# Layer two's mixing: a third block product computed as seven, with its kept sums made earlier in the kernel

## The chip, the core and the metric

The kernel runs on one core of a Trainium2 chip. The metric is the device time of one execution in microseconds (us); lower is better. The core has five engines with an instruction stream each: TensorE (PE, with weight loads shown as PEld), VectorE (DVE), ScalarE (ACT), GpSimd (POOL) and SyncE (SP), which here only issues DMAs. An engine runs its instructions in the order of the program and waits, where it must, for what another engine or a DMA delivers.

## The reference

Two layers, each a linear-attention block and a gated MLP that mixes over tokens, on x of 2048 tokens by 512:

```
def _A_ref(x, wqkv, wo):                      # 32 heads of 16
    qkv = (x @ wqkv) as (3, heads, tokens, 16)
    pq, pk = phi(q), phi(k)                   # t + 1 or exp(t), + 1e-6
    kv = einsum("bhsd,bhse->bhde", pk, v)
    z = einsum("bhsd->bhd", pk)
    o = einsum(pq, kv) / (einsum(pq, z) + 1e-6)
    return o @ wo

def _B_ref(x, w_in, w_sp, b_sp, w_out):       # F = 1792, Fh = 896
    z = gelu(x @ w_in)
    z1, z2 = z[..., :Fh], layernorm(z[..., Fh:])
    g = einsum("ts,bsf->btf", w_sp, z2) + b_sp[None, :, None]
    return (z1 * g) @ w_out

x = A_x
x = x + _A_ref(layernorm(x), A_wqkv, A_wo)
x = x + _B_ref(layernorm(x), B_w_in, B_w_sp, B_b_sp, B_w_out)
x = x + _A_ref(layernorm(x), A_wqkv, A_wo)
x = x + _B_ref(layernorm(x), B_w_in, B_w_sp, B_b_sp, B_w_out)
```

The costliest part is the mixing, `w_sp` (2048 x 2048) times `z2` (2048 x 896), once in each layer, with the same `w_sp`.

## The kernel before

**Arithmetic.** Each fp32 factor is split into a high part (a copy on ACT, `high`, L105) and a low part (a subtraction on DVE, `low`, L108), and a product is three matmuls: high by high, high by low, low by high (`mm3`, L119 to L121; in the mixing L1389 to L1391, and L1329, L1331 and L1332 in a nested product).

**Storage.** On-chip memory is cut into slots: 22 "pages" of 128 x 512 floats (`pg`), six "quads" four times as large (`qd`), four "bigs" (`bg`), tagged pages `z0` to `z15`, and eight accumulator banks. A slot is taken from a list of free ones and given back; whoever takes it next waits until its last reader is done.

**Order.** The program is scheduled by hand: each engine runs its instructions in the order of the code. Loops are over steps, and each step's code names the side work that it takes along. SP issues most DMAs, in order; the loads of kept sums are issued by POOL (L1193).

**Stages**, for each layer: the attention half (`P1`, steps of one token tile of 128), a transition and first half of the MLP (`P2`), the mixing, then the output loop `o` (16 steps, one token tile each, `z1 * g` times `w_out`), which in layer one also prepares layer two's start (`join`: loads of layer two's wk and wq, and of its first turned tiles, `turn.load`). The output tile is added on DVE and stored at L1515.

**The mixing as seven products.** The 2048 x 2048 by 2048 x 896 product is cut two by two, and instead of eight block products seven are computed, P1 to P7, whose operands are sums of blocks and whose results are added into the output. The list `ORDERS` gives the order for each layer. A plain product takes 8 steps, one for each 128 rows of the contraction: in P4, P1 and P5 (`WITH3`) a step has 24 matmuls, in P6, P7 and P3 it has 18. Each step needs one weight tile (fetched four steps ahead by `fetch`, split two steps ahead in `prepare`, ACT L1244 and DVE L1253) and one z tile (built in `operand`, split three steps ahead; L1257). When a product ends, `evac` adds its banks into the output or moves them (for instance L1443, six additions after P7).

**A nested product** ("N") is one of the block products taken once more as seven. N1 stands for P1 and N2 for P2; such a product has 14 steps with 12 matmuls. Seven sub-products (`NEST`) have two steps each. Those in `OWN` load a raw weight tile of 512 KB by SP and split it like the others; those in `SUM` load a sum of weight tiles that was computed earlier, split into high and low, and stored in device memory: 1 MB each, eight in one nested product. `nested_operand` takes its z side, from sums of z tiles made by `token_sums` (L1274, L1275) and others; the PSUM results are added into the output on DVE at each second step.

**Kept sums.** `Inner` makes these, in 16 units for a nested product. A unit is an addition or subtraction of two pages of raw weight (DVE, L1131 to L1141), then a high and a low part, then two stores of 256 KB each. Raw pages are loaded ahead by `Inner.fetch`. Two of these objects, N1 and N2, are served at named steps of `P2.run` and of the mixing (`MIX_UNITS`). The plain products' weight sums are made by another object on POOL (L1050) in layer one.

**Gates.** When a part of the output is complete it goes on the list `ready`; `gates` then loads a page of z1, and one step later multiplies it in on POOL (L1411). POOL also issues the sum loads, in the order of the code.

In layer one the order is P4, P1, P6, P7, P5, P3, N2; in layer two P4, P6, P7, N1, N2, P5, P3.

Of the kernel before, what the change touches and what calls it, by code (L numbers as in the profile page):

```python
# [29 lines left out]
MIX_UNITS = (11, 15, 18, 20, 25, 31, 36, 40), (7, 9, 11, 13, 15, 17, 19, 21)  # L30
# [3 lines left out]
class Slots:  # L34
# [16 lines left out]
    def put(self, *tiles):  # L51
        for t in tiles:
            n, _ = self.held.pop(id(t))
            self.free_list.append(n)


@with_exitstack
def mixer_kernel(ctx: ExitStack, tc: tile.TileContext, x_in, wqkv, wo_d, win1_d, win2_d, wsp_d, bsp_d, wout_d,
# [242 lines left out]
    class P1:  # L301
# [194 lines left out]
        def run(self):  # L496
            side = deque()
            for w in (self.wo, self.win2):
                side.extend([w] * len(w.pieces))
            self.wv = quads.get([P, 4, 512])  # L500
            ND = NT - DEFER
            for s in range(1, NT + 2):
                self.loadx(s + 3)
                self.turn.load(s + 1)
                turned = 2 <= s < NT and s not in self.turn.by_pe
                if turned:
                    self.T_high(s)
                if s == 1:
                    if not self.kb:
                        self.K(0)  # L510
                    self.K(1)
                elif 2 < s <= NT:
                    self.K(s - 1)
                self.ln_a(s + 2)
                if turned:
                    self.T_low(s)
                if s <= NT:
                    self.K_phi(s - 1)
                if s <= ND:
                    self.Q(s - 1)  # L520
                if s == NT + 1:
                    self.late()
                if s <= NT:
                    self.xsplit(s - 1)
                    self.K_split(s - 1)
                if s + 1 < NT and s + 1 in self.turn.by_pe:
# [8 lines left out]
                if s <= 4:  # L535
                    c = s - 1
                    nc.sync.dma_start(self.wv[:, c, :], wqkv[c * P:(c + 1) * P, 1024:1536])
                else:
                    for _ in range(min(len(side), 1 if s < 6 else 2)):
                        side.popleft().piece()  # L540
                if s >= 4:
                    for w in list(side)[:1 if s < 5 else 2]:
                        w.fetch()
# [72 lines left out]
    class P2:  # L616
# [309 lines left out]
        def run(self, sums):  # L926
            w1 = self.win1
            own = inner["N1" if self.seven else "N2"]
            for s in range(1, NT + 3):
# [28 lines left out]
                else:  # L958
# [19 lines left out]
                    if s <= NT + 1:  # L978
                        if not sooner:
                            self.d_high(s - 2)  # L980
                        if 6 <= s < 13 if self.seven else 14 <= s < 18:
                            own.unit()
                        self.d_low(s - 2)
# [87 lines left out]
    class Inner:  # L1071
# [3 lines left out]
        def __init__(self, base):  # L1075
            self.base = base
            self.d = {m: dram.tile([2, P, 2, 2, 512], F32, name=f"n{base}_{m}") for m in range(1, 5)}
# [4 lines left out]
            self.free = None  # L1082

        def part(self):
            if self.free is None:
                return pages.get(PAGE, F32R)
            i = self.free.popleft()
            self.free.append(i)
            return ztag(i, PAGE, "part", F32R)

        def fetch(self):

            if self.ahead:
                k, u = self.ahead.popleft()
                b = self.base
                at = (((3, b), (3, b + 4)), ((2, b),), (), ((2, b + 4),))[u]
                for name, (n, s) in zip(("21", "22") if u == 0 else ("11",) if u == 1 else ("12",), at):
                    self.raw[name] = load(wsp_d[n, s + k])

        def out(self):  # L1100
            for m, k, n, p in self.parts:
                nc.sync.dma_start(self.d[m][k // 2][:, k % 2, n, :], p.bitcast(F32))
                if id(p) in pages.held:
                    pages.put(p)
            self.parts = []

        def finish(self, late=False):
# [7 lines left out]
            if not keep:  # L1115
                pages.put(t)
            self.parts = [(m, k, n, p) for n, p in enumerate((h, l))]
# [31 lines left out]

        def begin(self, n, ahead=2):  # L1150
# [6 lines left out]
    class P4:  # L1157
# [4 lines left out]
        ORDERS = ("P4", "P1", "P6", "P7", "P5", "P3", "N2"), ("P4", "P6", "P7", "N1", "N2", "P5", "P3")  # L1162
# [4 lines left out]
        OWN = {"P1": (2, 0), "P2": (2, 4), "P4": (3, 4)}  # L1167
        SUM = {"P3": 4, "P5": 1, "P6": 2, "P7": 3}

        def __init__(self, p2, sums):  # L1170
# [11 lines left out]
            self.wout = {}  # L1182
            self.wraw = deque()
            self.wsteps = (48, 50, 51, 53, 55, 56, 57) if self.nest_late else range(60, 67)
            self.wloads = (45, 47, 48, 50, 52, 53, 54) if self.nest_late else range(60, 67)

        def fetch(self, g):
# [8 lines left out]
            if p[0] == "N":  # L1196
                n, s = self.OWN[self.NEST[k // 2]]
                s += 2 * (k % 2) + inner[p].base
# [8 lines left out]
        def operand(self, g):  # L1207
# [6 lines left out]
            if p == "P6":  # L1214
                return a[:, H2], -1.0, None
# [60 lines left out]

        def nested_operand(self, g):
            p, d = self.steps[g]
            name, q, base = self.NEST[d // 2], d % 2, inner[p].base
# [16 lines left out]
        def nested_low(self, g):  # L1296
# [7 lines left out]
            for o in range(2):  # L1304
                a, b = (ztile[inner[self.steps[g][0]].base + 2 * q + o + i] for i in (0, 4))
# [7 lines left out]
        def nested_mm(self, g):  # L1313
# [24 lines left out]
            V = nc.vector  # L1338
            for i in range(2):
# [21 lines left out]
            if name == "P4" and self.nest_late:  # L1361
                self.ready.extend((n, f, False) for n in (2, 3) for f in range(4))
# [56 lines left out]
        def evac(self, p):  # L1419
# [3 lines left out]
            if p in ("P4", "P1", "P5"):  # L1423
                for j in range(2):
                    n = 2 + j if p == "P1" else j
                    held = p == "P5"
# [4 lines left out]
            for j in range(2):  # L1431
                a, b = 2 + j, j
                for f in range(3):
# [8 lines left out]
                    elif p == "P7":  # L1442
                        V.tensor_sub(self.unit(b, 4 + f), bs[b], q)  # L1443
# [9 lines left out]
                    if p in ("P4", "P7", "P3"):  # L1453
                        banks.put(q)
            if self.L == 0:
# [24 lines left out]
        def wpiece(self, f):  # L1480
            r = self.wraw.popleft()
            h, l = (main.tile(PAGE, F32R, tag=f"z{2 * f + i}", bufs=1, name=f"wo{self.L}_{f}_{i}") for i in range(2))
# [5 lines left out]
        def loadx(self, i):  # L1488
            if i < NT:
                self.x[i] = load(xs[2 * self.L + 1, i])  # L1490

        def zsplit(self, i):
            if i >= NT:
                return
            n, k = divmod(i, 4)
# [5 lines left out]
        def o(self, i):  # L1501
# [7 lines left out]
            if self.L == 1 and i == NT - 1:  # L1509
# [11 lines left out]
        def run(self, nxt):  # L1521
# [16 lines left out]
            for m in ("N1", "N2"):  # L1538
                if (m, 0) in self.steps:
                    at = self.steps.index((m, 0))  # L1540
                    for k, g in enumerate(range(at - 3, at + 1) if m == "N1" or self.nest_late
                                          else (self.steps.index(("N1", s)) for s in (5, 6, 8, 9))):
                        sums_at[g] = m, k
            for g in range(n):
# [12 lines left out]
                if g == units[0] - 2:  # L1557
                    own.begin(len(units) // 4, 0)
                if g + 2 in units:
                    own.fetch()  # L1560
                if g in units:
                    own.unit(True)
                elif units[0] < g < units[-1] + 3:
                    own.finish(True)
                if g == 3:
                    self.loadb()
                if g in sums_at:
                    self.token_sums(inner[sums_at[g][0]].base, sums_at[g][1])
                if (p, k) == ("P5", 0) and not self.nest_late:
                    self.ready.extend((n, f, True) for n in range(2) for f in range(3))  # L1570
# [9 lines left out]
                if g == n - 1 and not self.nest_late:  # L1580
                    self.zsplit(0)
# [5 lines left out]
                if not self.nest_late and p == "P6" and k < 2:  # L1587
                    nc.vector.tensor_add(self.bs[k], self.bs[k], self.bs[2 + k])
# [5 lines left out]
            if not self.nest_late:  # L1594
                self.zsplit(1)
            make = Make() if nxt is not None else None
            for i in range(NT):
# [6 lines left out]
                self.o(i)  # L1604
                self.zsplit(i + 2)
                if make is not None:
                    make.step(i)
                if nxt is not None:
                    self.join(i, nxt)

        def join(self, i, nxt):
# [18 lines left out]
    inner = {p: Inner(b) for p, b in (("N1", 0), ("N2", 8))}  # L1630
# [44 lines left out]
```

## Time and profile before

| what | us |
|---|---|
| median of three runs | 1368.94 (1368.34, 1369.77, 1368.94) |
| profiled execution, span from first to last instruction | 1367.4 |
| PE busy | 1361.1 |
| DVE busy | 990.2 |
| ACT busy | 618.1 |
| POOL busy | 462.5 |

For the profiled execution only its span is known, 1367.4 us; its own time as the runs count it is not given, and the median of the runs lies 1.54 us above the span. Busy times are sums over the whole span. The mixing of layer one with its output loop ends at 691.26 us in this execution, layer two's attention half goes from there to about 809 us, its mixing starts at 1026.01 us (P4 of layer two to 1069.53), N1 of layer two is from 1134.81 to 1172.89 us. Matmuls are modelled with their pipelining, so a busy PE is a PE with work in it. DMA rates of the kernel: 209 GB/s over the span, in some stages near 380.

### The profile page before, as it was taken

How to read it: one execution, taken by the hardware profiler on the slowest of the kernel's cores; microseconds unless marked ns; L12 is line 12 of the kernel's file. 1: busy time of each engine (PE TensorE's matmuls, PEld its weight loads, DVE VectorE, ACT ScalarE, POOL GpSimd, SP SyncE). 2: the span in 40 equal slices, each digit the busy share in tenths (PEclk: the TensorE clock that was granted, in tenths of full speed). 3: DMA queues.
4: the chain of work that ended last, by engine and by line, in shares of the span. 5: the costliest groups of instructions: out<-in, count | busy, mean ns of one | idle time of the engine just before them, and what ended most of it. 6: DMA issues, size and time to landing. Idle time of an engine off the chain costs nothing.

```text
span 1367.4 us, 18070 instructions
## 1 busy us (share of the span) xinstructions
PE 1361.1 (100%) x6129; PEld 1141.0 (83%) x6129; DVE 990.2 (72%) x1471; ACT 618.1 (45%) x978; POOL 462.5 (34%) x537
## 2 busy tenths in 40 slices
PE   9999999999999999999999999999999999999998
PEld 7888888888888888888888888888888888888887
DVE  6775888765757789887667758887767578985742
ACT  6675544444443443441356655534454452442410
POOL 3333475433334137524123434543220001133350
PEclk9999999999999999999999999999999999999999
DMA  5542377877788988897944414777366569854452
GB/s 171 177 131 63 116 246 257 263 247 270 256 249 282 309 277 275 267 355 228 314 124 158 138 56 132 227 224 250 115 198 195 176 225 323 308 183 162 171 189 90
DMA packets 168957, 287.02 MB, mean 210 GB/s; under 512 B 14624, under 2 KB 58528, under 8 KB 165792
## 3 DMA queue, kind: packets, MB, share of 16 engines
q1 hardware_dynamic: 161808, 254.27, 57.7%
q0 software_dynamic: 5184, 28.31, 5.7%
q10 hardware_dynamic: 1872, 3.28, 0.6%
q8 instruction: 48, 0.79, 0.2%
q14 instruction: 45, 0.37, 0.1%
HBM read 196.94 MB, written 88.87 MB: 209 GB/s over the span
## 4 chain that ended last, share of the span: by engine, by line
PE 100%; DVE 0%; DVEq 0%; issue 0%
PE bank L121 19%; PE bank L120 19%; PE bank L119 19%; PE bank L1389 10%; PE bank L1390 10%; PE bank L1391 10%; PE bank L1329 3%; PE bank L1332 3%; PE bank L1331 3%; PE bank L840 1%; PE bank L841 1%; PE bank L839 1%; PE bank L257 1%; PE bank L580 1%; PE bank L445 0%; PE bank L476 0%
## 5 line engine op out<-in xcount | busy, mean ns | idle before, releaser
L1389 PE MATMUL bank<-qd,pg 128*128 128x512 f32 x608 | 236.5, 389 | 0.0
L1390 PE MATMUL bank<-qd,pg 128*128 128x512 f32 x608 | 236.5, 389 | 0.0
L1391 PE MATMUL bank<-qd,pg 128*128 128x512 f32 x608 | 236.5, 389 | 0.0
L1253 DVE TENSOR_TENSOR qd<-qd,qd 128x1024 fp32r<-128x1024 f32 x106 | 145.6, 1373 | 79.0 <-ACT qd L1244 78.4
L1244 ACT ACTIVATE qd<-qd 128x1024 fp32r<-128x1024 f32 x106 | 112.1, 1058 | 128.1 <-DVE qd L1253 52.6
L105 ACT ACTIVATE pg<-pg 128x512 fp32r<-128x512 f32 (+1 forms) x141 | 87.0, 620 | 165.7 <-DVE pg L296 49.4
L121 PE MATMUL bank<-qd,pg 128*128 128x512 f32 x380 | 148.4, 391 | 0.0
L234 POOL TENSOR_SCALAR rs<-mv 128x1 f32<-128x1 f32 x95 | 40.8, 430 | 305.1 <-DVE mv L232 304.7
L1050 POOL TENSOR_TENSOR pg<-pg,pg 128x512 f32<-128x512 f32 x64 | 95.9, 1499 | 135.8 <-DMA pg<-in_wsp_dram 106.4
L1391 PEld LDWEIGHTS bank<-qd,pg 128*128 128x128 f32 x608 | 114.1, 188 | 23.9
L1389 PEld LDWEIGHTS bank<-qd,pg 128*128 128x128 f32 x608 | 114.1, 188 | 23.7
L1390 PEld LDWEIGHTS bank<-qd,pg 128*128 128x128 f32 x608 | 114.1, 188 | 23.5
L1411 POOL TENSOR_TENSOR bg<-bg,pg 128x512 f32<-128x512 f32 x56 | 89.3, 1606 | 127.3 <-DMA pg<-z 123.0
L245 ACT ACTIVATE pg<-pg,nb,rs 128x512 f32<-128x512 f32 x63 | 51.1, 812 | 143.1 <-POOL nb L239 127.6
L119 PE MATMUL bank<-qd,pg 128*128 128x512 f32 x284 | 110.7, 390 | 0.0
L120 PE MATMUL bank<-qd,pg 128*128 128x512 f32 x284 | 110.6, 389 | 0.0
L108 DVE TENSOR_TENSOR pg<-pg,pg 128x512 fp32r<-128x512 f32 (+1 forms) x139 | 102.5, 739 | 11.1 <-DMA z<-pg 3.7
L119 PE MATMUL bank<-bg,qd 128*128 128x448 f32 x256 | 94.0, 367 | 0.0
L120 PE MATMUL bank<-bg,qd 128*128 128x448 f32 x256 | 93.6, 366 | 0.0
L121 PE MATMUL bank<-bg,qd 128*128 128x448 f32 x256 | 93.4, 365 | 0.0
L296 DVE STREAM_TRANSPOSE pg<-pg 128x512 f32<-128x512 f32 x79 | 85.4, 1081 | 9.9 <-DMA pg<-xt 3.4
L119 PE MATMUL bank<-wo,qd 128*128 128x512 f32 x224 | 87.1, 389 | 0.0
(192 smaller groups left out, 3053.9 us busy)
## 6 DMA issues: line engine op xcount, KB each, us to landing
qd<-s SPq DMA_DIRECT2D x64, 512.0 KB, 4.0
pg<-in_wsp_dram SPq DMA_DIRECT2D x96, 256.0 KB, 4.6
qd<-n POOLq DMA_DIRECT2D x24, 1024.0 KB, 7.9
qd<-in_wsp_dram SPq DMA_DIRECT2D x42, 512.0 KB, 4.4
s<-pg SPq DMA_DIRECT2D x64, 256.0 KB, 4.2
pg<-x SPq DMA_DIRECT2D x64, 256.0 KB, 3.6
n<-pg SPq DMA_DIRECT2D x60, 256.0 KB, 4.2
pg<-z SPq DMA_DIRECT2D x56, 256.0 KB, 4.1
```

The source lines that it names most:

```text
L105: nc.scalar.activation(h, src, AF.Copy)
L108: nc.vector.tensor_sub(l, src, h.bitcast(F32))
L119: nc.tensor.matmul(out, ah, bh, start=start, stop=False)
L120: nc.tensor.matmul(out, ah, bl, start=False, stop=False)
L121: nc.tensor.matmul(out, al, bh, start=False, stop=stop)
L1050: nc.gpsimd.tensor_tensor(t, a, b, op=OP.add)
L1244: nc.scalar.activation(wh, r, AF.Copy)
L1253: nc.vector.tensor_sub(wl, r, wh.bitcast(F32))
L1389: m(out, h[:, o], w[:, 0, j, :], start=start, stop=False, skip_group_check=True)
L1390: m(out, h[:, o], w[:, 1, j, :], start=False, stop=False, skip_group_check=True)
L1391: m(out, l[:, o], w[:, 0, j, :], start=False, stop=stop, skip_group_check=True)
L1411: nc.gpsimd.tensor_tensor(u, u, z1, op=OP.mult)
```

## The change

Layer two's mixing now goes P6, P7, N1, N2, P5, P3, N4. P4, which came first with 192 matmuls, is replaced by N4, a nested product of 168 placed last. Layer one's order is as it was.

- `Inner` gets three arguments (row block of the weight, base tile, base token tile), and a third object N4 with rows 0, base 8, tokens 0.
- N4's kept sums are new work: 16 units. Eight are made one a step in layer one's output loop (`early`, `O_UNITS`), eight in layer two's attention half (`A_UNITS`), both by the new `pooled`, which does the addition on POOL in one step, the high part on ACT in the next, the low part on DVE in a third and the two stores in a fourth. In the attention half its buffers come from two quads cut into pages (`Views`), so the load of wv comes later, and the pieces of wo and win2 are split one a step.
- N1's and N2's kept sums: those made in layer two (N1) use `pooled` too, from step 6 on in `P2.run` and at other steps of the mixing.
- P6's operand now does the addition that P4's did; P4's z operand is written in place during P5's steps (`fourth_operand`). The last parts of the output wait for N4, so the output loop takes token tiles 8 to 15 first, and w_out's pieces go to other tags and steps. Additions that followed P4 are made in other places (`bsum`, six copies on ACT in N2).
- `join` fetches two pieces of wk or wq a step in steps 8 to 11 instead of four in 8 and 10.

```diff
-MIX_UNITS = (11, 15, 18, 20, 25, 31, 36, 40), (7, 9, 11, 13, 15, 17, 19, 21)
+MIX_UNITS = (11, 15, 18, 20, 25, 31, 36, 40), (1, 3, 5, 7, 9, 11, 13, 15)
+O_UNITS = 7, 8, 9, 10, 11, 12, 13, 14
+A_UNITS = 1, 2, 3, 5, 6, 8, 9, 11
...
+            own = inner["N4"] if self.L == 1 else None
+            if own is not None:
+                spare = quads.get([P, 2, 2, 512]), quads.get([P, 2, 2, 512])
+                views = own.home = Views(pages, *spare)
+            else:
+                self.wv = quads.get([P, 4, 512])
+            each = 2 if own is None else 1
...
+                if own is not None and s <= NT:
+                    own.pooled(s in A_UNITS)
...
                     if s == 5:
                         own.begin(2)
-                    elif s in (8, 11):
-                        own.unit()
+                    elif 6 <= s:
+                        own.pooled()
...
+        def pooled(self, more=True):
+
+            self.out()
+            if self.open is not None:
+                m, k, h, t, keep = self.open
+                l = self.part() if keep else t
+                low(l if keep else t.bitcast(F32R), t, h)
+                if m == 4:
+                    self.home.put(self.S2)
+                self.parts = [(m, k, 0, h, True), (m, k, 1, l, True)]
+                self.open = None
+            if self.added is not None:
+                m, k, t, keep = self.added
+                h = self.part()
+                high(h if h.dtype == F32R else h.bitcast(F32R), t)
+                self.open, self.added = (m, k, h, t, keep), None
+            if not (more and self.due):
+                return
...
+            def op(t, a, b, o):
+                nc.gpsimd.tensor_tensor(t, a, b, op=o)
...
-        ORDERS = ("P4", "P1", "P6", "P7", "P5", "P3", "N2"), ("P4", "P6", "P7", "N1", "N2", "P5", "P3")
+        ORDERS = ("P4", "P1", "P6", "P7", "P5", "P3", "N2"), ("P6", "P7", "N1", "N2", "P5", "P3", "N4")
...
+            self.wloads = (45, 47, 48, 50, 52, 53, 54) if self.nest_late else (51, 53, 55, 56, 64, 66, 68)
+            self.wtags = list(range(14)) if self.nest_late else [*range(8, 16), *range(6)]
+            self.order = list(range(NT)) if self.nest_late else [*range(HT, NT), *range(HT)]
...
             if p == "P6":
+                if self.L == 1:
+                    nc.vector.tensor_add(a[:, H2], a[:, H2], b[:, H2])
                 return a[:, H2], -1.0, None
...
+        def fourth_operand(self, k):
+
+            a, b = ztile[k], ztile[k + HT]
+            nc.vector.tensor_sub(a[:, self.H1], a[:, self.H2], b[:, self.H1])
+            nc.vector.tensor_sub(a[:, self.H3], b[:, self.H3], a[:, self.H3])
...
+            if p == "N4":
+                for n, out in {"P1": ((1, self.X),), "P6": ((2, self.X),), "P2": ((1, self.Y),), "P5": ((4, self.Y),),
+                               "P7": ((4, self.X),), "P3": ((2, self.Y),), "P4": ((3, self.X),)}[name]:
+                    for i in range(2):
+                        f = i if n % 2 else 2 + i
+                        u = self.unit(n // 3, f)
+                        (V.tensor_add if f == 3 else V.tensor_sub)(u, u, out[i])
...
-            elif p in ("P5", "P3"):
-                self.ready.extend((n, f, False) for n, at in (((0, 3), (1, 3)) if p == "P5" else ((2, 0), (3, 0)))
-                                  for f in range(at, NF))
+            elif p in ("P5", "P3"):
+                self.ready.extend((n, f, False) for n in ((0, 1) if p == "P5" else (2, 3)) for f in range(4, NF))
...
+                if not self.nest_late:
+                    if g == 0:
+                        own.begin(2, 1)
+                    elif g <= units[-1] + 3:
+                        own.pooled(g in units)
...
+                if p == "P5" and not self.nest_late:
+                    self.fourth_operand(k)
...
+        def early(self, i):
+
+            own = inner["N4"]
+            if i == O_UNITS[0] - 2:
+                own.begin(4, 1)
+            elif i >= O_UNITS[0]:
+                own.pooled(i in O_UNITS)
...
-            if i in (8, 10):
-                for _ in range(4):
-                    (nxt.wk if i == 8 else nxt.wq).fetch()
+            if 8 <= i < 12:
+                for _ in range(2):
+                    (nxt.wk if i < 10 else nxt.wq).fetch()
...
-    inner = {p: Inner(b) for p, b in (("N1", 0), ("N2", 8))}
+    inner = {"N1": Inner(2, 0, 0), "N2": Inner(2, 8, 8), "N4": Inner(0, 8, 0)}
```

More of the change, by code (lines that the diff above doesn't have):

```diff
@@ L54, in put, with __init__, get, close @@
             self.free_list.append(n)
+class Views:
+    def __init__(self, pages, *tiles, holds=None):
+        self.pages = pages
+        self.free_list = deque(t[:, n // 2, n % 2] for n in range(4) for t in tiles)
+        self.held = {}
+        if holds is not None:
+            self.free_list, self.held = None, holds.held
+    def get(self, shape, dtype=F32):
+        if not self.free_list:
+            return self.pages.get(shape, dtype)
+        t = self.free_list.popleft()
+        self.held[id(t)] = t
+        return t
+    def put(self, t):
+        if id(t) not in self.held:
+            self.pages.put(t)
+            return
+        self.held.pop(id(t))
+        if self.free_list is not None:
+            self.free_list.append(t)
+    def close(self):
+        assert not self.held
 @with_exitstack
@@ L525, in run @@
                     self.K_split(s - 1)
+                if own is not None and s <= NT:
+                    own.pooled(s in A_UNITS)
+                    if s == A_UNITS[-2]:
+                        own.home = Views(pages, holds=views)
+                    if s == NT - 1:
+                        views.close()
+                        quads.put(*spare)
+                        self.wv = quads.get([P, 4, 512])
                 if s + 1 < NT and s + 1 in self.turn.by_pe:
@@ L1094, in fetch @@
                 k, u = self.ahead.popleft()
-                b = self.base
-                at = (((3, b), (3, b + 4)), ((2, b),), (), ((2, b + 4),))[u]
+                n, b = self.rows, self.base
+                at = (((n + 1, b), (n + 1, b + 4)), ((n, b),), (), ((n, b + 4),))[u]
                 for name, (n, s) in zip(("21", "22") if u == 0 else ("11",) if u == 1 else ("12",), at):
-                    self.raw[name] = load(wsp_d[n, s + k])
+                    self.raw[name] = t = self.home.get(PAGE)
+                    nc.sync.dma_start(t, wsp_d[n, s + k])
         def out(self):
[L1101 to L1104, printed above, removed]
+            for m, k, n, p, back in self.parts:
+                nc.sync.dma_start(self.d[m][k // 2][:, k % 2, n, :], p if p.dtype == F32 else p.bitcast(F32))
+                if back:
+                    self.home.put(p)
             self.parts = []
@@ L1115, in finish @@
             if not keep:
-                pages.put(t)
-            self.parts = [(m, k, n, p) for n, p in enumerate((h, l))]
+                self.home.put(t)
+            self.parts = [(m, k, n, p, self.free is None) for n, p in enumerate((h, l))]
             self.open = None
@@ L1454, in evac @@
                         banks.put(q)
+            if p == "P7" and self.L == 1:
+                pages.put(*self.bsum)
             if self.L == 0:
```

124 lines of the change are left out of this document (78 added, 46 removed).

## The prediction

> **What bounds the kernel now.** I read the page first (shares, chain, costliest groups), then TensorE's list of waits, then windows cut at the products of the mixing, then the DMA view and the timeline where the change puts work.
>
> ```profile
> span 1367.4 us, 18070 instructions
> PE 1361.1 (100%) x6129; PEld 1141.0 (83%) x6129; DVE 990.2 (72%) x1471; ACT 618.1 (45%) x978; POOL 462.5 (34%) x537
> PE 100%; DVE 0%; DVEq 0%; issue 0%
> L1389 PE MATMUL bank<-qd,pg 128*128 128x512 f32 x608 | 236.5, 389 | 0.0
> PE bank L445 <- DVE pg L440: 2.4, 1, 2.4
> 1026.01:1069.53 43.52, 43.52 (x193) 36.04 (x192) 27.50 (x45) 20.05 (x29) 0.00 (x0) 1.00 0.57 180
> 1134.81:1172.89 38.08, 38.08 (x169) 31.53 (x168) 34.00 (x64) 12.92 (x24) 4.23 (x8) 1.00 0.89 310
> 576.95:615.03 38.08, 38.08 (x169) 31.46 (x168) 32.69 (x50) 16.95 (x26) 9.61 (x11) 1.00 0.92 343
> ```
>
> TensorE (PE) is busy for 1361.1 of 1367.4 us, the chain that ended last is PE alone, and the list of its waits has one entry, 2.4 us near the start. So the time is the number of matmuls times their spacing, and every other engine and the DMAs matter only if they make PE wait. The last three rows are windows, with the columns stretch, length, busy time (and count) of PE, PEld, DVE, ACT, POOL, granted clock, DMA share, GB/s: P4 of layer two (the product that the change replaces), N1 of layer two and N2 of layer one (products of the kind that it adds). PE is busy without a gap in all three at clock 1.00. P4 is 192 matmuls in 43.52 us, 0.2267 us each; a nested product is 168 in 38.08 us, 0.2267 too. (The window counts one more that overlaps its edge.)
>
> **Matmuls.** P4 (8 steps of 24) goes and N4 (14 steps of 12) comes: 24 fewer, 24 x 0.2267 = 5.44 us, which is also 43.52 - 38.08. Nothing else on PE changes: its instruction list, as the program issues it, goes from 6014 rows to 5990. The profiled execution spans 1367.4 us and the median of the runs is 1368.94, so 1.54 us lie around the span and I carry them over. With no new wait: 1368.94 - 5.44 = 1363.50. All that remains is what PE will wait for.
>
> **Kept sums, first half, in layer one's output loop** (16 steps of 4.76 us, from 615.06 to 691.26).
>
> ```profile
> 638.86:681.70 42.84, 42.84 (x190) 35.47 (x189) 30.14 (x43) 14.17 (x20) 8.29 (x13) 1.00 0.93 310
> 681.70:691.26 9.56, 9.56 (x44) 7.92 (x43) 6.36 (x8) 3.12 (x5) 0.00 (x0) 1.00 0.17 65
> 648.38:653.14 4.76, 4.76 (x22) 3.94 (x21) 4.25 (x6) 0.82 (x2) 1.29 (x1) 1.00 1.03 380
> 674.67 0.71 SPq L101 DMA_DIRECT2D pg<-xt  x1
> 678.27 0.38 SPq L101 DMA_DIRECT2D pg<-xt  x1
> 687.27 1.08 DVE L296 STREAM_TRANSPOSE pg<-pg 128x512 f32<-128x512 f32 x1
> 689.04 0.69 DVE L108 TENSOR_TENSOR pg<-pg,pg 128x512 fp32r<-128x512 f32 x1 [0.70 <-ACT pg L105]
> 689.65 1.08 DVE L296 STREAM_TRANSPOSE pg<-pg 128x512 f32<-128x512 f32 x1
> 691.22 0.39 PE L119 MATMUL bank<-qd,pg 128*128 128x512 f32 x1
> pg<-xt SPq DMA_DIRECT2D x2, 256.0 KB, 5.4
> L1050 POOL TENSOR_TENSOR pg<-pg,pg 128x512 f32<-128x512 f32 x64 | 95.9, 1499 | 135.8 <-DMA pg<-in_wsp_dram 106.4
> L105 ACT ACTIVATE pg<-pg 128x512 fp32r<-128x512 f32 (+1 forms) x141 | 87.0, 620 | 165.7 <-DVE pg L296 49.4
> L108 DVE TENSOR_TENSOR pg<-pg,pg 128x512 fp32r<-128x512 f32 (+1 forms) x139 | 102.5, 739 | 11.1 <-DMA z<-pg 3.7
> ```
>
> Eight units, one a step from step 7: an add on POOL (L1050, the like of it, 1.50 us), a high part on ACT (0.62), a low part on DVE (0.74). Against 4.76 us a step, with DVE at most 70% busy over steps 5 to 13, that is covered. The DMAs are not obviously so: 10 loads and, within the loop, 12 stores, 22 pages of 256 KB. At 380 GB/s (the row with share 1.03) a page takes 0.69 us, so 15.2 us come; free are 7% of 42.84 plus 83% of 9.56, 10.9 us. The queues get 4.3 us longer than the loop, and SP issues in order. What PE needs from them are layer two's first turned tiles: issued 674.67, turned at 687.27, split by 689.73, used at 691.22 (1.5 us over); the second issued 678.27, turned at 689.65. Issue to use is 12.6 and 11.4 us, landing takes 5.4, so 7.2 and 6.0 us are spare before the transposes. Against these stand the 4.3 us and some five more DMAs ahead of the turned load in SP's order, 5 x 0.69 = 3.5 us: 7.8 us if all of it stands ahead, as against 7.2 + 1.5 and 6.0 + 1.5. Bounds 0 and about 0.5 us; I take 0, because stores and loads after the turned ones carry part of the 4.3. The wk and wq loads are only spread, two a step.
>
> **Second half, in layer two's attention half.** Eight units more, the wv load moved to step 15, the wo and win2 pieces one a step instead of two.
>
> ```profile
> 691.26:821.00 129.74, 129.74 (x592) 108.00 (x591) 88.57 (x146) 83.23 (x141) 44.92 (x59) 1.00 0.40 122
> ```
>
> DVE has 41 us free and DMA 60% of 129.74, 78 us, against 8 x 0.74 = 5.9 us on DVE, 8 x 0.62 on ACT, 8 x 1.50 on POOL and 26 pages (6 loads, 20 stores) x 0.69 = 17.9 us: cost 0. N1's adds that move from DVE (L1131 and its like) to POOL in the next halves lie under the same cover, as do the moved copies and adds of the edge units.
>
> **The start of the mixing.** P6 now comes first, with 18 matmuls a step, 4.08 us, in place of 24 and 5.44.
>
> ```profile
> 1032.27 0.55 DVE L1223 TENSOR_TENSOR z_z<-z_z,z_z 128x384 f32<-128x384 f32 x1
> 1032.85 0.56 DVE L1224 TENSOR_TENSOR pg<-z_z,z_z 128x384 f32<-128x384 f32 x1
> 1033.33 0.28 DVE L1225 TENSOR_TENSOR pg<-z_z,z_z 128x128 f32<-128x128 f32 x1
> 1033.53 1.22 DVE L1253 TENSOR_TENSOR qd<-qd,qd 128x1024 fp32r<-128x1024 f32 x1
> 1036.89 0.39 PE L1389 MATMUL bank<-qd,pg 128*128 128x512 f32 x1
> ```
>
> The weight of step 2 is split by 1034.75 and used at 1036.89, 2.1 us over; in P6's pace step 2 begins at 1026.01 + 2 x 4.08 = 1034.17, 2.7 us sooner. DVE gets there sooner too: three tensor operations of P4's operand a step (0.55 + 0.56 + 0.28 us) become one of some 0.55. Two steps save 2 x 0.84 = 1.7 us: 1.1 us over. Later P6 steps need 1.22 + 0.55 + 0.55 of DVE in 4.08 us. Cost 0, bound 0.5.
>
> **N4 itself, last.** Its eight kept sums come in on POOL's queue, 1 MB each.
>
> ```profile
> qd<-n POOLq DMA_DIRECT2D x8, 1024.0 KB, 10.1
> q0 software_dynamic: 1152, 8.39, 75.2%
> pg<-in_wout_dram SPq DMA_DIRECT2D x5, 256.0 KB, 6.6
> pg<-z SPq DMA_DIRECT2D x3, 256.0 KB, 8.9
> DMA to landing us min/median/max: 5.1/7.9/12.9
> 593.74 0.54 POOL L1193 DMA_DIRECT2D qd<-n  x1 [2.18 <-PE bank L1332]
> 606.88 0.39 PE L1329 MATMUL bank<-qd,pg 128*128 128x512 f32 x1
> L1411 POOL TENSOR_TENSOR bg<-bg,pg 128x512 f32<-128x512 f32 x56 | 89.3, 1606 | 127.3 <-DMA pg<-z 123.0
> 1131.61 4.09 DVE L1443 TENSOR_TENSOR bg<-pg,bank 128x512 f32<-128x512 f32 x6 [1.26 <-PE bank L1391]
> ```
>
> In N2 of layer one (577 to 606 us) these loads held 75.2% of the 16 DMA engines for 29 us, 21.8 us or 2.73 each, and a step of PE is 2.72 us: while they run there is no room. The last was issued at 593.74 for a use at 606.88, 13.14 us, and the longest landing of the kernel is 12.9: 0.2 us over, and PE did not wait. N4 has beside its sums six z1 pages (the gate factors of P3, one a step from its first), and three wout pages where N2 of layer one had five and three z1. Some two pages more stand ahead of the last sum, 2 x 0.69 = 1.4 us: a stall of 1.2 us, if layer one is the model. If N1 of layer two is (the same loads with no such neighbours), there is none. Bounds 0 and 1.2 plus what a late issue adds (first rival); I take 0.7, nearer to layer one. P3's six adds, done under N4's first step, run 4.1 us as P7's do now under N1's first step; N4's 14 bank adds are a fraction of what N1 does in 38.08 us with DVE at 34.00. Cost 0.
>
> The Trainium skill, "SBUF — State Buffer", section "A bandwidth-pool intuition that's wrong (but worth ruling out)", gives about 358 GB/s between HBM and a core. By that a sum would take 2.93 us and eight of them 1.6 us more, an estimate from that page, and the sum below would be 1365.8; the trace has 1048576 bytes in 2.73 us, 384 GB/s, and the trace decides.
>
> **Sum:** 1368.94 - 5.44 + 0 + 0 + 0 + 0.7 = 1364.2.
>
> **Rivals.** *First: gates hold the sums back, and it gets slower.* POOL issues the sum loads in order with the gate multiplications, and each of these waits for its z1 page, loaded one step before. Under full DMA the page takes 8.9 us and the multiplication 1.6. A sum that layer one issues 13.1 us ahead of its use, 1.17 steps after that page's step begins (use six steps later, 6 x 2.72 - 13.14 = 3.2 us), goes out at 8.9 + 1.6 = 10.5 us, 7.3 late. Then 5.8 us are left for a landing of up to 12.9: 7.1 us of stall, with the two pages 8.5, so 1363.50 + 8.5 = 1372.0. It decides as soon as z1 pages take over 3.2 - 1.6 = 1.6 us under load. Against it: a late issue also empties the queue, and the shortest landing, 5.1 us, still fits in 5.8. Chance 0.10.
>
> *Second: layer one's output loop is full.* The turned load waits not for 7.8 us but also for its page, which a sum's store must free:
>
> ```profile
> n<-pg SPq DMA_DIRECT2D x60, 256.0 KB, 4.2
> ```
>
> That is 7.8 + 4.2 = 12.0 against 7.5 us, a stall of 4.5 us before layer two's first K product: 1364.2 + 4.5 = 1368.7, no difference. For it: SP is in order and the share is already 0.93. Against: two loop steps at 0.17. Chance 0.14.
>
> *Third: POOL's adds stop DVE.*
>
> ```profile
> 566.71 1.61 POOL L1411 TENSOR_TENSOR bg<-bg,pg 128x512 f32<-128x512 f32 x1 [0.62 <-DMA pg<-z]
> 567.09 1.52 DVE L1274 TENSOR_TENSOR pg<-z_z 128x256 f32<-128x256 f32 x1
> 1126.02 0.42 DVE L1274 TENSOR_TENSOR pg<-z_z 128x256 f32<-128x256 f32 x1
> ```
>
> The same DVE operation takes 0.42 us alone and 1.52 beside a POOL one. So each of the adds put on POOL can cost DVE up to 1.5 us where it falls. Where DVE has over 1.5 us spare a step that is nothing; at the mixing's third step (1.1 us over) it is 0.4, and once or twice more with the gates of N4, 0.4 + 2 x 1.1 = 2.6: 1364.2 + 2.6 = 1366.8 at most. Chance 0.10. The Trainium skill, "SBUF — State Buffer", section "Who interferes with whom", says that a two-input VectorE operation and a GpSimd operation lock each other out of a shared port for a whole instruction; by that rule 1.5 us is the full price each time, and the two rows agree.
>
> That the change removes no matmul is excluded by the instruction list.
>
> **Chances.** Forecast 0.66, rivals 0.10, 0.14, 0.10. A measurement here tells some 0.2%, 2.7 us, from no change: faster below 1366.2, slower above 1371.7. Faster: 0.66 + 0.06 of the third + 0.03 of the second (a shorter stall) = 0.75. Slower: 0.08 of the first. Same: the rest, 0.17. The range begins 0.6 us under the value without any wait (the runs' own spread), at 1362.9, and reaches over the third rival and most of the second, to 1368.3.
>
> **What would show it.** Right: 24 fewer matmuls, the list of PE's waits with the old 2.4 us and under 1 us at N4's steps 9 to 12, the last sum landing within 1 us of its use, layer two's first K product at the same time as now. Wrong: a wait at layer two's first K product (second), POOL idle on z1 between sum issues with PE waiting at N4's fifth step already (first), DVE named as PE's releaser (third).

## The result and the profile after

The changed kernel takes 1380.45 us (median of four, 1379.07 to 1382.42) against 1369.36 before: a ratio of 1.0082, 95% interval 1.0067 to 1.0096. It is slower by 11 us where 4.7 us of gain were forecast, and above the forecast's range. The profiled execution took 1382.42 us with a span of 1380.7.

The page of the changed kernel:

```profile
span 1380.7 us, 18258 instructions
PE 1363.6 (99%) x6105; PEld 1136.6 (82%) x6105; DVE 1021.1 (74%) x1509; ACT 626.0 (45%) x1004; POOL 503.8 (36%) x571
```

The first six rows of its list of TensorE's waits (engine, tile and line <- releaser: us in total, times, longest):

```profile
PE bank L150 <- ACT z_h L136: 3.6, 2, 2.4
PE bank L150 <- ACT pg L136: 2.7, 1, 2.7
PE bank L476 <- DVE pg L471: 2.4, 1, 2.4
PE bank L152 <- DVE qd L139: 1.9, 1, 1.9
PE bank L1429 <- DMA qd<-n: 1.4, 2, 0.7
PE bank L883 <- DMA pg<-win_sums: 0.6, 1, 0.6
```

There are 24 fewer matmuls (6105 against 6129), as forecast; yet PE is busy for 2.5 us longer, and a list that had one entry has new ones. Matching the matmuls of both traces one by one gives where the 13.3 us of span came from. Up to 672 us, in layer one's output loop, hardly anything is shifted. Then PE's matmuls run later than before by 2.83 us at 684.98, by 5.81 at layer two's first K product, by 7.87 ten matmuls on, by 7.9 still at 785, by 14.46 at 807, by 16.06 at the start of layer two's mixing (of the 1.6 us between, 0.6 are a wait for loads of `win_sums`; no run takes the rest apart). The mixing takes back 5.44 and loses 2.9, of which N4 2.6: 13.5 at the end. The timeline rows that carry it:

```profile
684.94 0.33 SPq L132 DMA_DIRECT2D pg<-xt  x1
684.98 0.50 PE L152 MATMUL bank<-wo,qd 128*128 128x512 f32 x1 [1.92 <-DVE qd L139]
697.03 0.79 PE L150 MATMUL bank<-qd,pg 128*128 128x512 f32 x1 [2.67 <-ACT pg L136]
790.28 0.50 PE L150 MATMUL bank<-qd,z_h 128*128 128x512 f32 x1 [1.20 <-ACT z_h L136]
798.72 0.50 PE L150 MATMUL bank<-qd,z_h 128*128 128x512 f32 x1 [2.35 <-ACT z_h L136]
```

ACT's list of waits for 640 to 700 us has, first of all,

```profile
ACT pg L136 <- DMA n<-pg: 11.9, 2, 6.3
```

and two windows (columns as in the prediction):

```profile
681.82:697.03 15.21, 10.50 (x45) 7.73 (x43) 11.26 (x14) 5.79 (x10) 4.95 (x4) 1.00 0.97 340
697.03:700.35 3.32, 3.09 (x7) 1.99 (x7) 2.53 (x3) 0.84 (x2) 0.84 (x1) 0.51 0.78 234
```

The first turned tile is loaded at 684.94, 10.3 us later than before (674.67), and the first K product starts at 697.03 instead of 691.22. ACT twice stood still, 11.9 us in all, until a store of a kept sum (`n<-pg`) had landed, because the page that it was to write was still being read by that store. No such entry is in the list of before. In the second window, after the wait, PE's granted clock is 0.51 for 3.3 us, so that some seven matmuls take twice as long. PE falls back by another 2.06 us there (0.23 of them a further wait, for DVE), and by 2.16 after the wait at 798.72.

### The profile page after: what moved, and what is told of

It is laid out like the page before. It is cut to its first block, busy times and chain, and to the rows that moved or that the text cites. A ratio compares the mean times of both kernels' runs of the same rounds, so it can differ in the third digit from the quotient of the medians.

```text
span 1380.7 us, 18258 instructions
## 1 busy us (share of the span) xinstructions
PE 1363.6 (99%) x6105; PEld 1136.6 (82%) x6105; DVE 1021.1 (74%) x1509; ACT 626.0 (45%) x1004; POOL 503.8 (36%) x571
## 5 line engine op out<-in xcount | busy, mean ns | idle before, releaser
L1502 PE MATMUL bank<-qd,pg 128*128 128x512 f32 x544 | 211.8, 389 | 0.0
L1503 PE MATMUL bank<-qd,pg 128*128 128x512 f32 x544 | 211.7, 389 | 0.0
L1504 PE MATMUL bank<-qd,pg 128*128 128x512 f32 x544 | 211.7, 389 | 0.0
L1347 DVE TENSOR_TENSOR qd<-qd,qd 128x1024 fp32r<-128x1024 f32 x104 | 148.4, 1426 | 67.6 <-ACT qd L1338 67.0
L136 ACT ACTIVATE pg<-pg 128x512 fp32r<-128x512 f32 (+1 forms) x157 | 96.6, 620 | 184.5 <-DVE pg L327 56.0
L152 PE MATMUL bank<-qd,pg 128*128 128x512 f32 x380 | 150.3, 396 | 0.5 <-DVE pg L139 0.5
L139 DVE TENSOR_TENSOR pg<-pg,pg 128x512 fp32r<-128x512 f32 (+1 forms) x155 | 116.4, 753 | 16.9 <-DMA z<-pg 5.5
L1503 PEld LDWEIGHTS bank<-qd,pg 128*128 128x128 f32 x544 | 102.1, 188 | 21.5 <-DVE qd L1347 0.2
L1502 PEld LDWEIGHTS bank<-qd,pg 128*128 128x128 f32 x544 | 102.1, 188 | 21.4 <-ACT bg L1554 0.3
L1504 PEld LDWEIGHTS bank<-qd,pg 128*128 128x128 f32 x544 | 102.1, 188 | 21.1
L150 PE MATMUL bank<-qd,pg 128*128 128x512 f32 x284 | 111.4, 392 | 2.7 <-ACT pg L136 2.7
L151 PE MATMUL bank<-qd,pg 128*128 128x512 f32 x284 | 111.0, 391 | 0.0
L327 DVE STREAM_TRANSPOSE pg<-pg 128x512 f32<-128x512 f32 x79 | 85.3, 1080 | 12.1 <-issue 6.1
```

What stands on the lines that cost most here:

```text
L136: nc.scalar.activation(h, src, AF.Copy)
L139: nc.vector.tensor_sub(l, src, h.bitcast(F32))
L150: nc.tensor.matmul(out, ah, bh, start=start, stop=False)
L151: nc.tensor.matmul(out, ah, bl, start=False, stop=False)
L152: nc.tensor.matmul(out, al, bh, start=False, stop=stop)
L1347: nc.vector.tensor_sub(wl, r, wh.bitcast(F32))
```

## The experiments

The kernel before, measured again beside each group of runs, took 1368.92 to 1369.73 us.

The theory after the first look: the gain of 5.44 us is there, and it is lost where the kept sums are made, in two places for two reasons. The rivals: the new order (P6 first, N4 last) costs it, or each unit costs some time wherever it is.

**e1: no sums made.** N4 reads N2's kept sums.

```diff
-nc.gpsimd.dma_start(self.w[g], inner[p].d[...])
+nc.gpsimd.dma_start(self.w[g], inner["N2" if p == "N4" else p].d[...])
-own = inner["N4"] if self.L == 1 else None
+own = None
-self.early(i)
```

> N4 loads the kept sums of N2 instead of its own, and its own 16 units are not made at all (so the values of N4 are not those of the reference); order of the products, gates and everything else as in the changed kernel. Theory (the time is lost where the sums are made): PE's waits before the mixing go, N4's own of about 2 us stay: 1369.4 - 5.4 + 2 to 3 = 1366 to 1367. Rival (the time is lost by the new order, P6 first and N4 last): 1374 or more, with waits in the mixing.

Measured 1366.19 us (before 1369.14; ratio 0.998, 0.997 to 0.9989). Its list of waits:

```profile
PE bank L476 <- DVE pg L471: 2.4, 1, 2.4
PE bank L1429 <- DMA qd<-n: 1.7, 2, 1.5
PE bank L1502 <- ACT bg L1554: 1.0, 1, 1.0
```

All waits ahead of the mixing are gone but the old one near the start. The order of the products is not the cause; the making of the sums is, for 14.3 us (with it go the later load of wv and the single pieces). The wait for L1554 does belong to the new order: at P6's end ACT copies its banks, and P7 needs them. It is 1.0 to 1.5 us in e1, e4, e5 and e6; the changed kernel lost 0.2 us there, and the forecast had no such term.

**e2 and e3: one half of the units each.** e2 leaves out the attention half's, e3 the output loop's; N4 reads N2's for the missing half.

```diff
+inner["N2" if p == "N4" and k % 2 else p].d[...]
 e2: own = None in the attention half, begin(2, 1) in the loop
 e3: begin(2, 1) at i == 14 of the loop, no unit in it
```

> Only the eight units of layer one's output loop are made; N4 takes the other half of its sums from N2's (values not the reference's). Theory: the 7.9 us that the trace shows lost up to layer two's first K products come back, on top of the kernel without sums: about 1374, of which some 2 us are matmuls at half pace after the wait. Rival (the loop only shifts work, the loss is made up): 1367.

> Only eight units are made, all in layer two's attention half; N4 takes the other half of its sums from N2's (values not the reference's). Theory (each place costs for itself): the waits near steps 12 and 13 of the attention half stay, 6.6 us over the kernel without sums: about 1373. Rival (they are only a consequence of the late start of the attention half): 1367.

Measured 1374.91 (e2) and 1373.13 (e3). Over e1 that is 8.7 and 6.9 us, together 15.6, against 14.3 for both in the changed kernel: each place costs for itself. In e2's trace the waits are those of 684 and 697 us, in e3's those of steps 12 and 13, and ACT's list of e2 (640 to 700 us) has the same page wait:

```profile
ACT pg L136 <- DMA n<-pg: 12.5, 2, 6.7
```

PE's lists begin, in e2 and then in e3, with

```profile
PE bank L150 <- ACT pg L136: 3.0, 1, 3.0
```

```profile
PE bank L150 <- ACT z_h L136: 2.9, 2, 2.4
```

**e4: the loop's units moved to layer one's attention half,** the others to steps 1 to 8 without a gap (the last was in step 11).

```diff
+A_UNITS = (2, 3, 4, 5, 6, 7, 8, 9), (1, 2, 3, 4, 5, 6, 7, 8)
-own = inner["N4"] if self.L == 1 else None
+own = inner["N4"]
```

> All 16 units are made and used: eight in layer one's attention half (steps 2 to 9), eight in layer two's (steps 1 to 8, one step earlier each at the end), none in the output loop; buffers stay in the two spare quads to the end. Theory: both waits before the mixing go, N4's own stays: 1366 to 1368. Rival (the units cost by POOL and DVE wherever they are put): 1372 or more, with waits in both attention halves.

Measured 1377.26, not the theory's 1366 to 1368 but in the rival's range. Both attention halves now wait, as PE's list and DVE's timeline show:

```profile
PE bank L150 <- ACT z_h L136: 6.1, 7, 1.1
```

```profile
786.24 1.38 DVE L139 TENSOR_TENSOR bg<-pg,bg 128x512 fp32r<-128x512 f32 x1 [0.54 <-ACT bg L136]
787.54 1.07 DVE L327 STREAM_TRANSPOSE pg<-pg 128x512 f32<-128x512 f32 x1
```

The seven waits are in steps 12 to 15, where no unit is made any more. The two DVE rows suggest why: a piece of win2 (`bg<-pg,bg`) is split in front of the next tile's transposition. With one piece a step instead of two, the pieces run on into steps that last 5.44 us and not 8.16.

**e5 and e6: two pieces a step again,** in e4 and in the changed kernel.

```diff
-each = 2 if own is None else 1
+each = 2
```

> As the kernel with the units moved (e4), but wo and win2 again split two pieces a step, so that no piece is left for steps 11 to 15 of the attention half. Theory (in those short steps the piece's low part on DVE stands ahead of the next turned tile; seven waits of 1 us): they go, 1366 to 1368. Rival (the units themselves, POOL's adds beside DVE, cost it): 1374 or more, waits stay.

> The changed kernel with this one edit, two pieces a step. Theory: of the 6.6 us lost in layer two's attention half, some 4 to 6 come back, the output loop's 7.9 stay: 1375 to 1376. Rival: no difference, 1380.

Measured 1376.27 (e5) and 1381.31 (e6): neither comes back, so the pieces alone were not the cause. The waits move to the first two short steps and get longer (e5: three, 4.7 us in all). What is used up is a lead. A turned tile's high part (`z_h`, on ACT) is ready some time ahead of its first use on PE. Before, at the last long step and the first short one:

```profile
764.39 0.63 ACT L105 ACTIVATE z_h<-pg 128x512 fp32r<-128x512 f32 x1 [1.91 <-DVE pg L296]
770.10 0.39 PE L119 MATMUL bank<-qd,z_h 128*128 128x512 f32 x1
772.37 0.63 ACT L105 ACTIVATE z_h<-pg 128x512 fp32r<-128x512 f32 x1 [1.92 <-DVE pg L296]
775.54 0.39 PE L119 MATMUL bank<-qd,z_h 128*128 128x512 f32 x1
```

770.10 - 765.02 = 5.1 us, then 2.5. The same two in e8 (below; its attention half is e5's):

```profile
774.52 0.63 ACT L136 ACTIVATE z_h<-pg 128x512 fp32r<-128x512 f32 x1 [1.91 <-DVE pg L327]
775.36 0.40 PE L150 MATMUL bank<-qd,z_h 128*128 128x512 f32 x1
782.48 0.63 ACT L136 ACTIVATE z_h<-pg 128x512 fp32r<-128x512 f32 x1 [1.90 <-DVE pg L327]
783.17 0.50 PE L150 MATMUL bank<-qd,z_h 128*128 128x512 f32 x1 [1.91 <-ACT z_h L136]
```

0.2 us, then nothing: eight units took 4.9 us of lead. Where it goes can be read between one transposition of a turned tile and the next, before (L296) and in e8 (L327):

```profile
708.26 1.07 DVE L296 STREAM_TRANSPOSE pg<-pg 128x512 f32<-128x512 f32 x1
715.03 1.07 DVE L296 STREAM_TRANSPOSE pg<-pg 128x512 f32<-128x512 f32 x1
721.34 1.08 DVE L327 STREAM_TRANSPOSE pg<-pg 128x512 f32<-128x512 f32 x1
725.59 0.62 ACT L136 ACTIVATE qd<-qd 128x512 fp32r<-128x512 f32 x1
728.69 1.08 DVE L327 STREAM_TRANSPOSE pg<-pg 128x512 f32<-128x512 f32 x1
763.06 1.87 DVE L139 TENSOR_TENSOR bg<-pg,bg 128x512 fp32r<-128x512 f32 x2
```

Before, it is 6.77 us; in e8, 7.35. The unit's high part (725.59) stands in ACT's order ahead of operations that DVE waits for. In later steps, where two pieces of win2 are split as well, it is 8.16 us before (746.96 to 755.12) and 9.14 in e8 (755.71 to 764.85); there the pieces' low parts take 1.87 us (763.06) for 1.28 before (753.91), beside a unit's addition on POOL. So a unit makes a step of this chain some 0.5 to 1 us longer, though DVE and ACT are idle for a third of the stage. Their idle time is no room: before, from 691.26 to 821 us, DVE waits for ACT in 37 of its 41 idle us, and ACT for DVE in 36 of its 46. Nor is there a fixed price for a unit: with four, in steps 1 to 4 (e14, below), the two leads are 4.8 and 2.3 us.

**e7 and e11: the loop's pages.** e7 gives the loop's units pages from two large buffers that the loop has freed; e11 also puts the loads for layer two's start ahead of the units' DMAs.

```diff
+own.spare = [bigs.get([P, NF, 512])]      # a second at i == 8
+own.home = own.views = Views(pages)
+own.views.free_list.extend(own.spare[0][:, n] for n in range(NF))
 e11: join(i, nxt) before early(i)
```

> The changed kernel, but the units of the output loop take their pages from two large buffers that the loop has already freed, and not from the common 22 pages; SP's order and the DMAs are the same. Theory A (too few pages: ACT and SP wait for stores to land before a page is free): the loop's 7.9 us go down to 0 to 3, 1373 to 1375. Theory B (the DMA engines are full, 15 us of transfers into 11 of room): the turned tiles are as late as before, 1379 or more.

> e7 (output loop's units in freed large buffers) with the loads for layer two's start (wk, wq, turned tiles) issued before the units' stores and loads of the same loop step. Theory (what is left of the loop's cost is SP's order): layer two's first K product waits under 0.5 us, 1 to 3.5 us below e7 (1373.5 to 1376). Rival (the DMA engines are full at that point): as e7, 1377.

Measured 1377.02 (e7, above theory A's 1373 to 1375) and 1377.15 (e11, from 1373.54 to 1379.48; the rival's number). In e7's trace the wait for `n<-pg` is gone from ACT's list and the loop itself no longer stalls; layer two's first K product waits 1.53 us, where it waited 2.67 in the changed kernel behind a loop that was already 2.83 late:

```profile
692.98 0.50 PE L150 MATMUL bank<-qd,pg 128*128 128x512 f32 x1 [1.53 <-ACT pg L136]
```

The windows of the wait and of the time after it:

```profile
691.26:692.98 1.72, 0.19 (x1) 0.00 (x0) 1.02 (x3) 0.63 (x1) 0.00 (x0) 1.00 1.05 404
692.98:696.50 3.52, 3.52 (x10) 2.56 (x11) 2.82 (x4) 1.26 (x2) 1.30 (x1) 0.72 0.94 350
```

PE is 3.7 us late after it, 2 of them at the lower clock (second window, 0.72), instead of 7.9. So the page shortage was about half of the loop's cost (3.4 us by the medians, of the 8.7 of e2; 4.2 of 7.9 by the traces). The DMA share is 1.05 at that wait, which would fit full DMA engines as the rest; it is not shown. e11's profiled execution, 1373.54 us, has no wait there, but its other runs go up to 1379.48, and the median is e7's: that SP's order is the rest is not shown either. What differs between its runs is left open.

**e8 and e10: gates held back in N4's first seven steps,** in e5 and in e1.

```diff
-if not (self.nest_late and 49 <= g < 57):
+if not (49 <= g < 57 if self.nest_late else 60 <= g < 67):
```

> e5, and the gates held back in the first seven steps of N4, so that neither their z1 pages nor their multiplications stand between the sum loads. Theory (the gates make N4's sums late): N4's waits of 0.4 to 2 us go, 1365 to 1367, 0.4 to 2 below e5. Rival (the DMAs' own rate does): no difference to e5.

> e1 (no units, N4 reads N2's kept sums, values not the reference's) with the gates held back in N4's first seven steps. Theory (N4's own waits come from the gates between the sum loads): 0.5 to 1.5 us below e1, 1364 to 1365.5, no wait in N4. Rival (DMA rate): as e1.

Measured 1374.70 (e8, 1.6 below e5) and 1366.49 (e10, as e1, above its 1364 to 1365.5). In the changed kernel POOL stood between the sum loads and waited for z1:

```profile
1276.31 1.49 POOL L1524 TENSOR_TENSOR bg<-bg,pg 128x512 f32<-128x512 f32 x1 [2.91 <-DMA pg<-z]
1282.66 1.29 POOL L1524 TENSOR_TENSOR bg<-bg,pg 128x512 f32<-128x512 f32 x1 [4.31 <-DMA pg<-z]
1283.90 0.59 POOL L1284 DMA_DIRECT2D qd<-n  x1
```

With the gates held, e8's trace has no wait for `qd<-n` at all, and e10's has one, of 0.2 us, in layer one. The mechanism is shown by the traces; in the times it is 1.6 us once and nothing once, since e10 lost some 2 us elsewhere (0.9 of them waits for the loads of `win_sums`).

**e9: fewer in a row.** Four units in each attention half, eight in P5 of layer two, two pieces a step, gates held.

```diff
+A_UNITS = (2, 3, 4, 5), (1, 2, 3, 4)
+P_UNITS = 44, 45, 46, 47, 48, 49, 50, 51
+elif P_UNITS[0] <= g <= P_UNITS[-1] + 3:
+    inner["N4"].pooled(g in P_UNITS)
```

> As e8, but only four units in each attention half (layer one steps 2 to 5, layer two steps 1 to 4), the other eight one a step in P5 of layer two, none in the output loop. Theory (in the attention half a unit lengthens the chain ACT to DVE of its step, and the lead of some five steps is used up by eight): no wait over 1 us before the mixing; P5 has DMA share 0.45 and DVE at 34.5 of 43.6 us, room for 22 pages (15 us) and eight low parts (5.5 us): 1364 to 1366. Rival (units cost about 0.7 us each wherever they are): 1372 or more.

Measured 1367.82 (1363.89 to 1373.34), above its 1364 to 1366. The attention halves no longer wait; P5 does, in the profiled execution, the slowest of the ten:

```profile
PE bank L1504 <- DVE bg L1563: 3.6, 1, 3.6
```

and its timeline ahead of that:

```profile
1201.34 0.53 ACT L1345 ACTIVATE pg<-z_z 128x384 fp32r<-128x384 f32 x1 [3.65 <-DMA n<-pg]
1202.97 1.66 DVE L1376 TENSOR_TENSOR z_z<-z_z,z_z 128x384 f32<-128x384 f32 x1
1210.26 0.55 DVE L1376 TENSOR_TENSOR z_z<-z_z,z_z 128x384 f32<-128x384 f32 x1
```

Again a page that a store still reads, and a DVE operation of 0.55 us that takes 1.66 beside a unit's addition on POOL (1202.44 to 1204.22).

**e12 and e13: four units in each of four places; or eight of them in the output loop.** In both the loop's units come earlier, from step 4, in freed large buffers.

```diff
 e12: P_UNITS = 44, 46, 48, 50, and pooled(i <= 7) in loop steps 4 to 10
 e13: no P_UNITS, and pooled(i <= 11) in loop steps 4 to 14
```

> All 16 units made and used, four in each of four places: layer one's attention half (steps 2 to 5), layer one's output loop (steps 4 to 7, buffers in a freed large one), layer two's attention half (steps 1 to 4), P5 of layer two (every second step); gates held back in N4, two pieces a step. Theory (each place has a lead that a few units don't use up, and what eight in a row cost is the lead used up): no wait over 1.5 us anywhere, 1364 to 1366, faster than before. Rival (each unit costs some 0.6 us in any number): 1373.

> As e12, but the four units of P5 go into the output loop too: eight there, steps 4 to 11, in two freed large buffers. Theory A (the loop's DMA engines have no room for 22 pages by the time that the turned tiles are loaded): waits of 2 to 5 us before layer two's first K products, 1368 to 1371. Theory B (only pages and SP's order were short): as e12, 1364 to 1366.

Measured 1368.97 (e12) and 1371.64 (e13), before 1368.92: both above their numbers. In e12's trace everything but the loop is free; the loop loses 3.9 us, at steps 10 to 12. The rows that lead there:

```profile
648.28 1.28 DVE L140 TENSOR_TENSOR pg<-pg,pg 128x512 fp32r<-128x512 f32 x2
657.32 2.38 DVE L140 TENSOR_TENSOR pg<-pg,pg 128x512 fp32r<-128x512 f32 x2
662.49 0.82 ACT L277 ACTIVATE pg<-pg,nb,rs 128x512 f32<-128x512 f32 x1 [6.11 <-POOL nb L271]
663.21 0.93 ACT L137 ACTIVATE qd<-bg 128x896 fp32r<-128x896 f32 x1
```

and PE's list has

```profile
PE bank L151 <- ACT qd L137: 1.0, 1, 1.0
```

Two low parts on DVE that take 1.28 us at 648.28 take 2.38 at 657.32, beside a unit's addition on POOL. DVE falls behind, then the layernorm that it feeds (`nb`, L277), and behind that, in ACT's order, the split of the loop's next operand (`qd`). How much of the 3.9 us is due to the longer operations is not measured. Four more units (e13) cost 2.7 us more. Its trace loses 6.2 us at steps 10 to 12 of the loop and 0.5 before layer two's K products, so its theory A named the wrong place.

**e14: none in the output loop.** Eight units at every second step from N2's step 10 of layer two on; the rest as in e12.

```diff
+P_UNITS = 40, 42, 44, 46, 48, 50, 52, 54
```

> As e12, but the four units of the output loop go elsewhere too: eight units, one every second step, from N2's step 10 to P3's step 2 of layer two; none in the output loop; four in each attention half; gates held in N4. All sums are made and used. Theory (e12's 3.9 us are the loop's, where DVE runs late beside POOL's adds, and the other places are free at this density): 1364 to 1365.5, faster than before by about the 5.4 us of matmuls less 0.5 to 1. Rival (the mixing has no room for eight units, as in e9): 1367 or more, with a wait at P5's end.

Measured 1365.25 us (1364.00 to 1368.55) against 1369.11: ratio 0.9976, 0.9967 to 0.9985. All 16 units are made and used, and it beats both kernels. The head of its page, and its list of waits, almost that of before:

```profile
span 1363.4 us, 18269 instructions
```

```profile
PE bank L477 <- DVE pg L472: 2.4, 1, 2.4
PE bank L508 <- ACT pg L137: 0.4, 1, 0.4
PE bank L153 <- DVE pg L140: 0.3, 1, 0.3
PE bank L1431 <- DMA qd<-n: 0.2, 1, 0.2
```

## Why the prediction was wrong

- **Matmuls, -5.44 us: right.** 24 fewer, and e14, the same products with the sums elsewhere, gives 3.9 us of it net.
- **Start of the mixing, 0: right.** In the changed kernel PE waits neither at step 2 nor later in P6; what P6's end can cost (e1) was not weighed.
- **N4, 0.7 us: the mechanism was the first rival's, its size was not.** POOL did wait on z1 between the sum loads, and PE for the last sums; matched matmul by matmul N4 loses 2.6 us. The 8.5 of the rival did not come: the last sum, issued at 1283.90, was used at 1292.36, so it landed within 8.5 us and not the 12.9 that the rival took. Layer one was no model for N4, since N2's gates are held back there already (`49 <= g < 57` in both kernels).
- **Output loop, 0: this step failed.** The sum weighed 15.2 us of transfers against 10.9 of room and SP's order, and let the stores behind the turned loads carry the rest. The second rival had the true mechanism, a page held by a store, but put it at one load, at 4.5 us. It holds ACT too (11.9 us), thereby the loop's own operands, and 7.9 us are lost, some 1.8 of them at the lower clock, which no step had. About half is the pages (e7); the cause of the rest stays open.
- **Attention half, 0: this step failed too.** It set 5.9 us of DVE work against 41 us free in the whole stage. The idle time of DVE and ACT there is mostly their waiting for one another, so each unit lengthens a step's chain, and eight use up the lead. It cost 6.6 us by the trace, and no rival spoke of it. The single pieces move the waits to other steps; that they add to the time is not shown (e5 and e6).
- **Third rival (POOL's adds stop DVE):** the prolonged DVE rows are there in e8, e9 and e12. It was priced at three operations. In e8 it is 0.6 us in such a step; in the loop and in P5 its share was not measured by itself.

## What to carry to other kernels

Idle share is not room where two engines hand work to and fro: measure the lead (ready to first use) at the tightest step of the stage, and compare it with what the added operations take from it. When stores are added, count the pages that they hold until they land, since whoever writes those pages next waits in order. Work that can be done at any time belongs where operands are prepared steps ahead, a little at a time: the same 16 units cost 14 us in one spread and under 2 in another (e14, with the gates held back).

## What was not expected of the hardware

A wait of PE costs more than its length. After waits of 2.67 us (changed kernel), 2.35 (there) and 1.53 (e7) the matmuls started every 0.43 us instead of 0.2267 for a time, which ended 3.3 to 4.9 us after the wait, about 2 us lost each time; after one of 1.92 us (684.98) they did not, but after waits of 1.9 us in e6 (686.12) and e8 (783.17) they did. The Trainium skill, "TensorE: Matmul & The Clock Gate", section "HAM oscillation — how this bites in real kernels", warns of idle gaps above about 3.4 us; here shorter ones were enough. The Trainium skill, same page, section "Part 1: The HAM clock gate (the "warmup" mystery)", says that the activity window runs freely, which would fit that waits of like length differ; no run here tested the window itself.
